# A check of the softmax sums moved onto TensorE, the zeros of two V tiles shared out, and a new written order

## The chip, the cores and the metric

The kernel runs on one core of one Trainium2 chip. The metric is the device time of one execution in microseconds; lower is better. The engines are TensorE (PE in the profile, its weight loads PEld), VectorE (DVE), ScalarE (ACT), GpSimd (POOL) and SyncE (SP, which issues nearly all DMAs).

## The reference

Two branches work on the same normalized input and are added to it:

```python
def _A_ref(x, wqkv, wo):            # attention: 32 heads of 16, window of 256 keys
    qkv = (x @ wqkv).reshape(B, S, 3, H, Dh).transpose(2, 0, 3, 1, 4)
    scores = einsum('bhqd,bhkd->bhqk', q, k) * Dh ** (-0.5)
    mask = (idx[:, None] - idx[None, :] >= 0) & (idx[:, None] - idx[None, :] < W)
    p = softmax(where(mask, scores, -1e9))
    return einsum('bhqk,bhkd->bhqd', p, v).transpose(0, 2, 1, 3).reshape(B, S, D) @ wo
def _B_ref(x, w_in, w_sp, b_sp, w_out):   # gated MLP with a mix over positions
    z = gelu(x @ w_in)
    z1, z2 = z[..., :Fh], layernorm(z[..., Fh:])
    g = einsum('ts,bsf->btf', w_sp, z2) + b_sp[None, :, None]
    return (z1 * g) @ w_out
xn = layernorm(x)
return x + _A_ref(xn, wqkv, wo) + _B_ref(xn, w_in, w_sp, b_sp, w_out)
```

S = 2048, D = 512, Fh = 688; all in bf16.

## The kernel before, in words

The tokens are 16 tiles of 128. A first part (to 83 us) normalizes x, makes z1 and z2 of all tiles and most of q, k and v. The part that matters here follows. It walks a string, `ORDER`, step by step, and issues for each step the instructions of all engines; each engine then runs its own in that sequence, held only by semaphores. So the string is the schedule. Its steps are:

- `q`, `g`, `f` and a number: begin the next qkv unit (4 matmuls of 512 columns), the next half tile of the position mix (`gf`, 16 matmuls of 344 columns, L588), or the next output tile (`fo`, 6 matmuls with uT and 4 with oT), and issue so many of its matmuls. A bare number goes on with the unit that is open.
- `S`: scores of one set, two PSUM score tiles of two banks each (`slot_mms`, L761), their exps by ScalarE into a tile `E` (L840) and the window masks by GpSimd's affine_select (L855). `A`, `B` and `T` do the same for three score tiles, the third copied by VectorE (L838), and open or close an output tile whose matmuls are issued one at a time by `y`.
- `D`: scores of the corners of the window (tile `ED`, L790); `d` masks them on VectorE (L862).
- `p`: P times V (`pv`, L727) for one block J of 256 queries and one group G of 8 heads, into a PSUM bank; VectorE turns it (`ot`, L734). `n` normalizes on VectorE: reciprocal of the sums into `r_all` (L740), product (L742), turn into `oT` (L750).

There are three score tiles in PSUM (`ps_s`), and two banks (`x_tile`) that gf, fo, o and the last qkv units share in turn. A bank comes free when VectorE has read it: into u (L602), xo (L627), ot (L734) or v_y (L168). uT comes from u by a DMA transpose, as do the weights wspT of tile t+2.

`pv` reads V through v_y, and for the corners through one of two tiles `vh0` and `vh1`, each loaded by two DMAs per block (`load_half`, L547 and L549) into half of its rows; the other half must be zero. `late()` closes the pool of xnT and the qkv weights, opens a pool in its place, and has GpSimd write these zeros (L539, L540). It is called by the first `D` or `p`.

The softmax is made without the maximum. At the end the kernel checks that every sum in `r_all` lies between 2^-60 and 2^40; if not, `attention_with_maximum` does the work again. `check_sums` counts the good sums of each partition (L873, L874), and a DMA brings the 128 counts into one row (L879). `least_sum`, called in `f_end` ahead of the last half tile's addition, takes the least of them (L886), and `make_flag` writes the flag (L892) after all steps. Every engine loads the flag into a register (L897) and branches (L1104). The last output tile is made in two halves of 256 columns; its second half is sent by ScalarE's queue.

Of the kernel before, what the change touches and what calls it, by code (L numbers as in the profile page):

```python
# [8 lines left out]
P = 128  # L9
BF = mybir.dt.bfloat16  # L10
F32 = mybir.dt.float32
ACT = mybir.ActivationFunctionType
ALU = mybir.AluOpType

S_TOK = 2048
D = 512
# [3 lines left out]
VROW = H * VW + DH  # L20
# [3 lines left out]
NB = S_TOK // P  # L24
NC = D // P
NG = 4
NJ = NB // 2
# [10 lines left out]
PAD = 64  # L38
# [4 lines left out]


ORDER = """
S q4 q2 S 2 q4 S q4 g7 D 9 S g10 S d 6 p S g5 n 11 D p p S p g7 D 5 n 3 d 1 g3 n 4 B y1 1 n y1 2
y1 3 y1 1 y1 2 A y3 g3 y1 5 d 2 B 5 y4 1 y2 A y1 g3 y1 2 y1 11 S p p D g12 S 4 n n g6 S 10 S p p
S g5 n 3 n 8 B y5 g1 y1 1 d y1 2 A 2 y1 5 y1 5 D p p D g4 n d 12 B n y2 g1 y1 1 y1 1 y1 3 A y1 1
y1 4 y1 1 y1 4 S p p S g8 n 6 d 2 B y4 g3 y1 1 n 3 A 1 y1 3 y3 5 D p p S g4 n 4 d 8 B y3 n g1 y1
3 y1 2 y1 A 1 y1 5 y2 4 D p p D g2 n 11 n 3 B y3 g3 d y1 1 y1 2 A 3 y2 1 y1 2 y1 4 S p p D g5 n  # L50
8 d 3 B y6 p A y2 d g11 y1 1 S 4 p n S p g6 n D 10 S p g6 n n 5 B y2 1 y1 3 y1 1 y1 d y4 T y8 n
y1 A g16 S p p D n g2 n 13 B y2 1 y4 d y3 T y9 A g16 D p p S g12 D d 4 g6 n S 8 n 2 S p p S g10
D n 4 n 2 f6 S 3 d 1 g7 S 9 S p p S g4 d 9 S n 3 g11 n 5 p p n f7 n 3 f10 f10 f10
"""


# [16 lines left out]
def kernel(  # L73
# [12 lines left out]
    nc = tc.nc  # L86
# [4 lines left out]
    pers = ctx.enter_context(tc.tile_pool(name="pers", bufs=1))  # L91
# [18 lines left out]
    xnT = pq.tile([P, NC, PAD + S_TOK], BF, name="xnT")  # L110
    wqkv = pq.tile([P, NC, 3 * D], BF, name="wqkv")
    r_all = pers.tile([P, NJ * NG, 16], F32, name="r_all")
    flag = pers.tile([P, 1], mybir.dt.int32, name="flag")
    wspp = ctx.enter_context(tc.tile_pool(name="wspp", bufs=2))
    sm = ctx.enter_context(tc.tile_pool(name="sm", bufs=4))
# [60 lines left out]
    with ExitStack() as actx:  # L176
        ps_s = actx.enter_context(
            tc.tile_pool(name="psa_s", bufs=2, space=bass.MemoryType.PSUM)
        )
# [49 lines left out]
        for w in WARM:  # L229
# [5 lines left out]
        nc.vector.memset(warm[:], 0.0)  # L235
        one = pa.tile([P, H], BF, name="one")
        nc.vector.memset(one[:], 1.0)
        nc.scalar.activation(out=warm[:, 0:4], in_=warm[:, 4:8], func=ACT.Gelu_apprx_tanh)
        make_identity(nc, ident[:])
        nc.vector.reduce_sum(  # L240
            out=hmask[:],
            in_=ident[:].rearrange("p (s e d) -> p e s d", s=4, e=2),
            axis=mybir.AxisListType.XY,
# [286 lines left out]
    def late():  # L530
        if not late_pool:
            assert not work["q"]
            pq_ctx.close()
            late_pool.append(
                late_ctx.enter_context(tc.tile_pool(name="late", bufs=1, side="right"))
            )
            for i in range(2):
                vh = late_pool[0].tile([P, 4, VROW], BF, name=f"vh{i}")
                nc.gpsimd.memset(vh[PAD:P, 0:2, :], 0.0)  # L539
                nc.gpsimd.memset(vh[0:PAD, 2:4, :], 0.0)  # L540
                v_half.append(vh)
        return late_pool[0]

    def load_half(J):
        late()
        vh = v_half[J % 2]
        nc.sync.dma_start(out=vh[0:PAD, 0:2, :], in_=v_y[0:PAD, 2 * J + 1 : 2 * J + 3, :])  # L547
        src = v_y[PAD:P, 2 * J - 2 : 2 * J, :] if J > 0 else v_y[0:PAD, 1:3, :]
        nc.sync.dma_start(out=vh[PAD:P, 2:4, :], in_=src)  # L549
# [72 lines left out]

    def f_end(t, c0, w, fo):
        xo = xos[t]
        if t == NB - 1 and c0 > 0:
            least_sum()
        nc.vector.tensor_tensor(  # L627
            out=xo[:, c0 : c0 + w], in0=fo[:, 0:w], in1=xo[:, c0 : c0 + w], op=ALU.add
        )
        eng = nc.scalar if c0 else nc.sync  # L630
        eng.dma_start(out=out2[t * P : (t + 1) * P, c0 : c0 + w], in_=xo[:, c0 : c0 + w])
        if not (rows or units or later):
            check_sums()
# [40 lines left out]
    def f_work(t, c0):  # L674
        if c0 == 0 and t + 2 < NB:
            load_xo(t + 2)
        w = f_cols(t)
        fo, _ = x_tile([P, 512], F32, "fo")
        for ch in range(NFC):
            nc.tensor.matmul(  # L680
                fo[:, 0:w], lhsT=uTs[t][:, ch, :], rhs=w_out_sb[:, ch, c0 : c0 + w],
                start=(ch == 0), stop=False,
            )
            yield
        q0 = t % 2 * P
        for c in range(NC):
            nc.tensor.matmul(  # L687
                fo[:, 0:w], lhsT=oTs[t // 2][:, c, q0 : q0 + P], rhs=wo_sb[:, c, c0 : c0 + w],
                start=False, stop=(c == NC - 1),
            )  # L690
            yield
        f_end(t, c0, w, fo)
# [75 lines left out]
    def do_corners(J, G):  # L768
        S = [ps_s.tile([P, 2, 512], F32, name="S", tag="S") for _ in range(2)]
        ED[(J, G // 2)] = late().tile([P, 32, PAD], BF, name="ED", bufs=2)  # L770
        if G == 0 and J == 0:
            load_half(0)
        if G == 2 and J + 1 < NJ:
            load_half(J + 1)
        Ed = ED[(J, G // 2)]
        for g in range(2):
            for t in range(2):
                i = 2 * J + t
                for strip in range(2):
                    late_q = strip == 0 or J == 0  # L780
                    k0 = i * P + P if late_q else i * P - 3 * PAD
                    q0 = i * P + PAD * late_q
                    gk = G + g + (2 * strip if J == 0 else 0)
                    for s in range(4):
                        o = S[s // 2][
                            strip * PAD : strip * PAD + PAD, s % 2, g * 256 : g * 256 + 256
                        ].rearrange("p (e t q) -> p e t q", e=2, t=2)[:, :, t, :]
                        score_mm(s, o, J, gk, k0, PAD, q0, PAD)
        for i in range(2):
            nc.scalar.activation(  # L790
                out=Ed[:, 16 * i : 16 * i + 16, :],
                in_=S[i][:].rearrange("p b (x q) -> p (b x) q", q=PAD),
                func=ACT.Exp, scale=SM_SCALE,
            )
# [73 lines left out]
    def check_sums():  # L868
        assert not (later or units)
        r = r_all[:].rearrange("p a b -> p (a b)")  # L870
        ok = ep.tile([P, 512], BF, name="ok", tag="E")
        low = ep.tile([P, 1], F32, name="low", tag="E")
        nc.vector.tensor_scalar(out=ok[:], in0=r, scalar1=R_LOW, scalar2=None, op0=ALU.is_ge)  # L873
        nc.vector.scalar_tensor_tensor(  # L874
            out=ok[:], in0=r, scalar=R_HIGH, in1=ok[:], op0=ALU.is_le, op1=ALU.mult,
            accum_out=low[:],
        )
        row = ep.tile([P, P], F32, name="row", tag="E")
        nc.sync.dma_start(out=row[0:1, :], in_=low[:])  # L879
        rows.append(row)  # L880

    lows = []

    def least_sum():
        low = sm.tile([P, 1], F32, name="low")
        nc.vector.tensor_reduce(  # L886
            out=low[0:1, :], in_=rows[0][0:1, :], axis=mybir.AxisListType.X, op=ALU.min
        )
        lows.append(low)

    def make_flag():
        nc.vector.tensor_scalar(  # L892
            out=flag[0:1, :], in0=lows[0][0:1, :], scalar1=16.0 * NJ * NG, scalar2=None, op0=ALU.is_lt
        )

    def read_flag():
# [177 lines left out]
    for step in ORDER.split():  # L1074
        if step in "STABCH":
            n = 2 if step == "S" else 1 if step == "H" else 3
            do_slots(n, step in "TA", step in "TB")
        elif step == "D":
            do_corners(*corners.pop(0))
        elif step == "d":  # L1080
            mask_corners(*masks.pop(0))
        elif step == "p":
            pv(*units.pop(0))
        elif step == "n":
            normalize(*later.pop(0))
        elif step[0] == "y":
            for _ in range(int(step[1:])):
                half_mm()
        else:
            if step[0] in work:  # L1090
                assert left == 0
                item = work[step[0]].pop(0)
                left, unit = (NFC + NC, f_work(*item)) if step[0] == "f" else item
                step = step[1:]
            for _ in range(int(step)):
                next(unit)
                left -= 1
            if left == 0:
                assert next(unit, None) is None
    assert not (left or slots or corners or masks or units or later or half)  # L1100
    assert not any(work.values())
    make_flag()
    late_ctx.close()
    with tc.If(read_flag() > 0):  # L1104
        with ExitStack() as gctx:
# [28 lines left out]
```

## Time and profile before

| | |
|---|---|
| Runs of the kernel before | 255.33, 255.51 and 256.52 us; median 255.51 |
| Profiled execution | 255.79 us, of which the span from the first to the last instruction is 254.0 |
| Busy | PE 247.7, ACT 195.6, DVE 200.1, POOL 105.3 us |
| TensorE clock granted | 0.999 |

A row of the chain of waits gives start, duration, engine, what it writes and its line; a row of the timeline adds shapes and a count, with the idle time before it and its releaser in square brackets. A row of the groups ends with busy time in us, mean ns of one, and idle time before. Matmuls overlap, so their recorded durations run past the start of the next; the distance from one stretch's start to the next one's is what the stretch costs.

### The profile page before, as it was taken

What the parts mean: (1) busy time and instruction counts of PE and PEld (TensorE: products, weight loads), DVE (VectorE), ACT (ScalarE), POOL (GpSimd) and SP (SyncE); (2) the same over time, 40 slices, a digit from 0 to 9 for tenths busy, and PEclk for the clock granted to TensorE, in tenths of its full rate; (3) what the DMA queues carried; (4) which work ended last, traced back from release to release, by engine and by line L of the source; (5) the groups of instructions that cost most, each with busy time, mean ns of one, the idle gap of its engine ahead of it and who ended that gap; (6) DMA issues with size and microseconds to landing.
All of it is one profiled execution on the core that took longest, in us unless ns stands there. A gap on an engine that the chain in (4) does not pass through costs nothing.

```text
span 254.0 us, 8684 instructions
## 1 busy us (share of the span) xinstructions
PE 247.7 (97%) x3712; PEld 141.3 (56%) x3712; DVE 200.1 (79%) x434; ACT 195.6 (77%) x234; POOL 105.3 (41%) x165
## 2 busy tenths in 40 slices
PE   7899999999999999999999999999999999999994
PEld 3555555555555356546557556566565464664653
DVE  7699977875657659985698898887998989684883
ACT  3756567556546998898989989889898899998900
POOL 3221211210010387575464465626484547543710
PEclk9999999999999999999999999999999999999999
DMA  6899722018400128646567717569184557675232
GB/s 198 291 252 195 195 54 31 1 41 104 105 1 0 44 46 122 143 124 137 54 86 181 131 44 189 50 157 157 38 168 41 138 77 126 117 101 125 36 54 69
DMA packets 67162, 26.82 MB, mean 106 GB/s; under 512 B 57040, under 2 KB 65584, under 8 KB 67120
## 3 DMA queue, kind: packets, MB, share of 16 engines
q1 hardware_dynamic: 66400, 25.50, 52.4%
q10 hardware_dynamic: 720, 0.73, 0.9%
q8 instruction: 30, 0.49, 0.9%
q14 instruction: 12, 0.10, 0.1%
HBM read 8.46 MB, written 2.10 MB: 42 GB/s over the span
## 4 chain that ended last, share of the span: by engine, by line
PE 92%; DMA 3%; DVE 2%; ACT 1%; issue 1%; SPq 0%; DVEq 0%
PE gf L588 31%; PE zp L370 14%; PE S L761 11%; PE fo L662 10%; PE o L727 9%; PE pj_o L143 6%; PE pj_f L143 5%; PE pj_o L161 3%; PE pj_f L161 2%; DMA w_in_sb<-in_B_w_in_dram 2%; DMA row<-low 1%; DVE xo L627 1%; PE fo L680 1%; PE zo L370 0%; PE fo L687 0%
## 5 line engine op out<-in xcount | busy, mean ns | idle before, releaser
L855 POOL TENSOR_SCALAR_AFFINE_SELECT E<-E 128x512 bf16<-128x512 bf16 x124 | 86.3, 721 | 68.0 <-ACT E L840 64.8
L840 ACT ACTIVATE E<-S 128x1024 bf16<-128x1024 f32 x102 | 97.6, 1027 | 9.1 <-PE S L761 9.0
L588 PE MATMUL gf<-z2n,wspT 128*128 128x344 bf16 x512 | 88.4, 310 | 0.0
L588 PEld LDWEIGHTS <-wspT 128*128 128x128 bf16 x512 | 47.4, 98 | 30.9 <-issue 5.9
L302 POOL TENSOR_TENSOR rs<-ve,mhalf 128x2 f32<-128x2 f32 (+1 forms) x18 | 12.1, 670 | 68.2 <-DVE ve L299 67.6
L370 PE MATMUL zp<-w_in_sb,xnT 128*128 128x344 bf16 x224 | 36.9, 309 | 0.1
L761 PE MATMUL S<-qpad,kT 32*64 32x128 bf16 (+2 forms) x848 | 32.0, 259 | 0.2 <-ACT E L840 0.2
L790 ACT ACTIVATE ED<-S 128x1024 bf16<-128x1024 f32 x30 | 29.1, 1024 | 1.6 <-PE S L761 1.5
L370 PEld LDWEIGHTS <-xnT 128*128 128x128 bf16 x224 | 21.6, 98 | 14.6 <-ACT xnT L361 0.7
L602 DVE SCALAR_TENSOR_TENSOR u<-gf,b_all,z 128x344 bf16<-128x344 f32 (+3 forms) x50 | 20.4, 438 | 11.7 <-PE gf L588 11.5
L734 DVE STREAM_TRANSPOSE ot<-o 128x512 f32<-128x512 f32 x32 | 22.5, 714 | 7.8 <-PE o L727 7.6
L838 DVE CAST E<-S 128x1024 bf16<-128x1024 f32 x22 | 26.7, 1213 | 2.2 <-PE S L761 2.2
L840 ACT ACTIVATE E<-E 128x1024 bf16<-128x1024 bf16 x22 | 23.4, 1063 | 0.8 <-DVE E L838 0.6
L727 PE MATMUL o<-E,v_y 128*32 128x128 bf16 (+1 forms) x736 | 23.5, 239 | 0.2
L761 PEld LDWEIGHTS <-kT 32*64 32x64 bf16 (+1 forms) x848 | 12.9, 99 | 18.6 <-issue 16.4
L727 PE MATMUL o<-ED,vh 128*32 128x64 bf16 x960 | 21.2, 193 | 0.0
L154 DVE TENSOR_SCALAR qpad<-qt,hmask 128x512 bf16<-128x512 bf16 x32 | 9.7, 348 | 13.6 <-ACT qt L152 13.6
L143 PEld LDWEIGHTS <-wqkv 128*128 128x128 bf16 x128 | 12.5, 98 | 12.8 <-DMA xnT<-xt 0.3
L862 DVE TENSOR_TENSOR ED<-ED,maskC 128x2048 bf16<-128x2048 bf16 x15 | 19.2, 1278 | 0.0
L378 ACT ACTIVATE z<-zp 128x688 bf16<-128x688 f32 x14 | 10.4, 743 | 10.9 <-PE zp L370 10.9
L143 PE MATMUL pj_o<-xnT,wqkv 128*128 128x512 bf16 x72 | 18.5, 379 | 0.0
L378 ACT ACTIVATE z2n<-zp 128x688 bf16<-128x688 f32 x14 | 10.4, 743 | 10.1 <-PE zp L370 10.1
(88 smaller groups left out, 306.7 us busy)
## 6 DMA issues: line engine op xcount, KB each, us to landing
vh<-v_y SPq DMA_DIRECT2D x16, 140.0 KB, 4.4
xo<-in_A_x_dram SPq DMA_DIRECT2D x16, 128.0 KB, 2.9
out_dram<-xo SPq DMA_DIRECT2D x15, 128.0 KB, 2.0
wqkv<-in_A_wqkv_dram SPq DMA_DIRECT2D x1, 1536.0 KB, 8.7
xt<-in_A_x_dram SPq DMA_DIRECT2D x2, 512.0 KB, 3.9
w_in_sb<-in_B_w_in_dram SPq DMA_DIRECT2D x5, 172.0 KB, 5.5
w_out_sb<-in_B_w_out_dram SPq DMA_DIRECT2D x1, 640.0 KB
w_in_sb<-in_B_w_in_dram ACTq DMA_DIRECT2D x3, 172.0 KB, 6.0
```

Source lines behind the costliest of these rows:

```text
L143: nc.tensor.matmul(pt[:], lhsT=wqkv[:, c, w0 : w0 + P], rhs=xnT[:, c, t0 : t0 + 512], start=(c == 0), stop=(c == NC - 1),)
L370: nc.tensor.matmul(out, lhsT=src[:, c, t0 : t0 + P], rhs=w_in_sb[:, c, f0 : f0 + HALF], start=(c == 0), stop=(c == NC - 1),)
L378: nc.scalar.activation(out=dst.rearrange("p (j f) -> p j f", j=2), in_=zp[:, :, 0:HALF], func=ACT.Gelu_apprx_tanh, scale=rsx[n] if n < 2 e ...
L588: nc.tensor.matmul(gf[:, 0:HALF], lhsT=wspT[t][:, c, :], rhs=z2n[:, c, j * HALF : (j + 1) * HALF], start=(c == 0), stop=(c == NB - 1),)
L662: nc.tensor.matmul(h["fo"][:], lhsT=lhsT, rhs=rhs, start=False, stop=(h["jobs"] == 2 and h["pos"] == NFH))
L727: nc.tensor.matmul(o[32 * s : 32 * s + 32, c0 + r0 : c0 + r0 + n], lhsT=v[:, m, h * VW : h * VW + 32], rhs=rhs(s), start=(i == 0), stop=(i ...
L734: nc.vector.transpose(out=ot[:].rearrange("p b j -> p (b j)"), in_=o[:])
L761: nc.tensor.matmul(out, lhsT=kT[32 * s : 32 * s + 32, g, k0 : k0 + nk], rhs=qpad[J // 2][32 * s : 32 * s + 32, g, :, qs - q00 : qs - q00 + ...
L790: nc.scalar.activation(out=Ed[:, 16 * i : 16 * i + 16, :], in_=S[i][:].rearrange("p b (x q) -> p (b x) q", q=PAD), func=ACT.Exp, scale=SM_ ...
L838: nc.vector.tensor_copy(out=part, in_=src)
L840: nc.scalar.activation(out=part, in_=src, func=ACT.Exp, scale=SM_SCALE)
L855: nc.gpsimd.affine_select(out=cells[:, :, k, :], in_=cells[:, :, k, :], pattern=pattern, compare_op=op, fill=0.0, base=base, channel_multi ...
```

## The change

- The row transfer and the least are gone. `check_sums` makes a column `bad` of 128 ones and zeros, and `make_flag` is called within the last half output tile, between its six uT matmuls and its four oT matmuls: a matmul with `bad` as weights and a column of ones counts the bad partitions into one element of a score tile, and VectorE compares that with 0.5.
- The zeros of vh0 are written by VectorE when `late()` opens the pool, those of vh1 by GpSimd at the corner step of block 1. `late()` is called when the last qkv unit is done.
- The string is another one, with the same units in another sequence.

```diff
 ORDER = """
-S q4 q2 S 2 q4 S q4 g7 D 9 S g10 S d 6 p S g5 n 11 D p p S p g7 D 5 n 3 d 1 g3 n 4 B y1 1 n y1 2
-y1 3 y1 1 y1 2 A y3 g3 y1 5 d 2 B 5 y4 1 y2 A y1 g3 y1 2 y1 11 S p p D g12 S 4 n n g6 S 10 S p p
-S g5 n 3 n 8 B y5 g1 y1 1 d y1 2 A 2 y1 5 y1 5 D p p D g4 n d 12 B n y2 g1 y1 1 y1 1 y1 3 A y1 1
-y1 4 y1 1 y1 4 S p p S g8 n 6 d 2 B y4 g3 y1 1 n 3 A 1 y1 3 y3 5 D p p S g4 n 4 d 8 B y3 n g1 y1
-3 y1 2 y1 A 1 y1 5 y2 4 D p p D g2 n 11 n 3 B y3 g3 d y1 1 y1 2 A 3 y2 1 y1 2 y1 4 S p p D g5 n
-8 d 3 B y6 p A y2 d g11 y1 1 S 4 p n S p g6 n D 10 S p g6 n n 5 B y2 1 y1 3 y1 1 y1 d y4 T y8 n
-y1 A g16 S p p D n g2 n 13 B y2 1 y4 d y3 T y9 A g16 D p p S g12 D d 4 g6 n S 8 n 2 S p p S g10
-D n 4 n 2 f6 S 3 d 1 g7 S 9 S p p S g4 d 9 S n 3 g11 n 5 p p n f7 n 3 f10 f10 f10
+S q4 q4 q1 S 3 q4 D g8 S 8 g1 S 2 d 9 S 4 p S p g4 n 4 S 8 p D p g9 D 6 n 1 g2 n 6 B y1 3 y3 n 5
+y1 A y2 g2 y2 3 d 5 B 1 y1 2 y2 1 y1 2 y3 A g5 y1 5 y1 6 S p d p S g9 n 3 S 4 g6 S 6 n 4 D p p S
+g14 n 1 n 1 B y5 g2 d 3 y1 1 A y2 2 y1 8 D p p D g6 n n 10 B y2 g2 y1 2 d 4 y1 A y2 2 y1 1 y1 1
+y1 4 S p n p S g11 n 5 B y3 d g1 y1 1 y1 2 y1 A 4 y1 3 y1 1 y1 4 D p p S g10 n 3 n 3 B y2 g1 y1
+6 d y1 2 A y2 1 y2 2 y1 4 D p p D g7 n n 9 B y2 g1 y1 1 d y2 3 y1 A 3 y2 4 y1 4 S p p D g15 d 1
+B y4 n y1 p A y3 g4 y1 3 d 6 S 3 p n n S p g5 S 11 D p g5 n 2 d 2 B 4 y2 3 y6 n y1 T y6 n y3 A
+g16 S p p n D g4 n 11 B y1 1 y8 T y1 d y8 A g16 D p p S g2 n 1 d 9 n 1 D 3 g6 S 10 S p p S g4 n
+9 D 1 d 2 d g5 S 7 n 4 f2 S 8 S p n p S g4 n 7 S 5 p g11 n 5 p f4 n 6 f10 f10 f10
 """
...
+    one1 = pers.tile([P, 1], BF, name="one1")
...
+        nc.vector.memset(one1[:], 1.0)
...
             for i in range(2):
-                vh = late_pool[0].tile([P, 4, VROW], BF, name=f"vh{i}")
-                nc.gpsimd.memset(vh[PAD:P, 0:2, :], 0.0)
-                nc.gpsimd.memset(vh[0:PAD, 2:4, :], 0.0)
-                v_half.append(vh)
+                v_half.append(late_pool[0].tile([P, 4, VROW], BF, name=f"vh{i}"))
+            clear_half(nc.vector, 0)
         return late_pool[0]
+
+    def clear_half(eng, i):
+        eng.memset(v_half[i][PAD:P, 0:2, :], 0.0)
+        eng.memset(v_half[i][0:PAD, 2:4, :], 0.0)
...
     def f_end(t, c0, w, fo):
         xo = xos[t]
-        if t == NB - 1 and c0 > 0:
-            least_sum()
...
             yield
+        if c0 > 0:
+            make_flag()
         q0 = t % 2 * P
...
         if G == 0 and J == 0:
             load_half(0)
+        if G == 0 and J == 1:
+            clear_half(nc.gpsimd, 1)
...
-        row = ep.tile([P, P], F32, name="row", tag="E")
-        nc.sync.dma_start(out=row[0:1, :], in_=low[:])
-        rows.append(row)
-
-    lows = []
-
-    def least_sum():
-        low = sm.tile([P, 1], F32, name="low")
-        nc.vector.tensor_reduce(
-            out=low[0:1, :], in_=rows[0][0:1, :], axis=mybir.AxisListType.X, op=ALU.min
-        )
-        lows.append(low)
+        bad = ep.tile([P, 1], BF, name="bad", tag="E")
+        nc.vector.tensor_scalar(
+            out=bad[:], in0=low[:], scalar1=16.0 * NJ * NG, scalar2=None, op0=ALU.is_lt
+        )
+        rows.append(bad)
 
     def make_flag():
+        count = ps_s.tile([P, 2, 512], F32, name="S", tag="S")[0:1, 0, 0:1]
+        nc.tensor.matmul(count, lhsT=rows[0][:], rhs=one1[:], start=True, stop=True)
         nc.vector.tensor_scalar(
-            out=flag[0:1, :], in0=lows[0][0:1, :], scalar1=16.0 * NJ * NG, scalar2=None, op0=ALU.is_lt
+            out=flag[0:1, :], in0=count, scalar1=0.5, scalar2=None, op0=ALU.is_ge
         )
...
             if left == 0:
                 assert next(unit, None) is None
+                if not work["q"]:
+                    late()
     ...
     assert not any(work.values())
-    make_flag()
```

## Prediction

> **What bounds the kernel now.** I read the page first: the span and the chain that ended last.
>
> ```profile
> span 254.0 us, 8684 instructions
> ...
> PE 92%; DMA 3%; DVE 2%; ACT 1%; issue 1%; SPq 0%; DVEq 0%
> PE gf L588 31%; PE zp L370 14%; PE S L761 11%; PE fo L662 10%; PE o L727 9%; PE pj_o L143 6%; PE pj_f L143 5%; PE pj_o L161 3%; PE pj_f L161 2%; DMA w_in_sb<-in_B_w_in_dram 2%; DMA row<-low 1%; DVE xo L627 1%; PE fo L680 1%; PE zo L370 0%; PE fo L687 0%
> ```
>
> The reader is to see that 92% of the chain is TensorE. A written order can then gain in only three ways: TensorE does less, TensorE waits less, or what comes after its last matmul gets shorter. So I looked in the chain of waits for the pieces that show what a stretch costs when nothing holds it. A score visit is one letter S of the order; a PV visit is one or two p in a row; the rest is full-array matmuls.
>
> ```profile
> 91.52 0.33 PE S L761 x4
> ...
> 117.29 1.46 PE o L727 x112
> ...
> 121.29 1.56 PE gf L588 x10
> ...
> 126.87 2.44 PE gf L588 x16
> ...
> 188.23 0.79 PE o L727 x56
> ...
> 198.70 2.05 PE fo L662 x9
> ```
>
> A gf matmul costs (2.44 - 1.56)/6 = 0.147 us, and a stretch of them has 1.56 - 1.47, some 0.1 us, on top. That is the change between full-array and tiled matmuls. An fo or qkv matmul is (2.05 - 0.1)/9 = 0.217. Two PVs together take 1.46 and one alone 0.79, so the second costs 0.67 and each visit some 0.12 beside its matmuls. Priced like this, most of the old order between 100 and 240 us comes out with nothing left over: TensorE hardly waits there. Its waits are at the two ends of the attention.
>
> ```profile
> 83.56 1.47 PE L161 MATMUL pj_f<-wqkv,xnT 128*128 128x512 bf16 x6
> 84.96 0.39 PE L761 MATMUL S<-qpad,kT 32*128 32x512 bf16 x2
> 85.53 0.39 PE L761 MATMUL S<-qpad,kT 32*128 32x512 bf16 x2 [0.19 <-ACT E L840]
> ```
> ```profile
> 87.33 0.43 PE S L761 x8
> ...
> 98.46 1.16 PE o L727 x64
> 99.62 0.40 PE S L761 x4
> 100.01 0.56 PE o L727 x32
> ```
>
> The second S visit began at 84.96, and half of it had to wait to 85.53 for the first exp, which frees a score buffer: 0.57 lost. The third took 0.43 in place of 0.33 (0.1). At 98.46 two first-block PVs take 1.16; one takes 0.56, so the two should take 0.56 + 0.56 - 0.12 = 1.00, and 0.16 is waiting; the next S has 0.07 more. GpSimd explains these two, in the timeline:
>
> ```profile
> 91.59 1.03 POOL L539 MEMSET vh<- 64x1120 bf16 x1
> ...
> 95.80 3.88 POOL L855 TENSOR_SCALAR_AFFINE_SELECT E<-E 128x512 bf16<-128x512 bf16 x6
> ```
>
> The four zero fills start at 91.59, with the masks next at 95.80: three sets stand queued behind the fills until 99.68, just what those PVs read. At the other end the pair of last PVs is held once more, and then the row transfer decides:
>
> ```profile
> 242.13 0.85 PE o L727 x56
> ...
> 243.01 0.90 PE o L727 x56
> ...
> 248.72 1.93 DMA row<-low
> ...
> 250.68 0.28 DVE low L886
> ```
>
> From 242.13 to 243.91 is 1.78, against 1.46 for a free pair: 0.3.
>
> **The change, part by part.** *The order on TensorE, own work.* All letters but the run of the p are as many as before. Counted in the two orders, p p stands 13 times before and 11 after, so the PVs are made in 21 visits and not 19, and the two extra ones cut full-array stretches in two. Each costs 0.12 + 0.1: **+0.45**.
>
> *The order, waits.* After the first S the new order puts nine qkv matmuls and not six: 83.56 + 9 x 0.217 + 0.1 = 85.61, later than 85.53, where the buffer comes free, so the 0.57 goes. The third use is now the corner step D, after 3 + 4 matmuls (1.6 us) where six stood; the 0.1 goes as well. What is late next is the bank of the qkv tiles, which a cast on VectorE frees; that goes into the new waits below. The PVs of block 0 come one by one behind S or D, with no zero fills ahead of their masks: -0.23. The final pair is parted by 11 gf matmuls (1.6 us, more than the turn of o on VectorE): -0.3. Sum **-1.2**.
>
> A small wait in the middle has a plain cause, and I have no reason to think that a tight order has fewer of them:
>
> ```profile
> 184.71 1.68 DVE L862 TENSOR_TENSOR ED<-ED,maskC 128x2048 bf16<-128x2048 bf16 x1
> ...
> 187.04 0.12 PEld L727 LDWEIGHTS <-v_y 128*32 128x32 bf16 x8 [0.43 <-DVE xo L627]
> ```
> ```profile
> L862 DVE TENSOR_TENSOR ED<-ED,maskC 128x2048 bf16<-128x2048 bf16 x15 | 19.2, 1278 | 0.0
> ```
>
> A mask of 1.68 in place of the mean 1.28 made an xo late, and with it the bank of the next PV. The new order packs exps, masks and turns as closely elsewhere: I add 0.2 (between 0 and 1) for waits that did not exist.
>
> *Zeros of the V tiles.* Buffer 0 is cleared by VectorE as soon as the last qkv unit is evicted, buffer 1 by GpSimd at the corner of block 1.
>
> ```profile
> L260 DVE MEMSET v_y<- 64x272 uint32 x1 | 0.3, 285 | 0.0
> ```
> ```profile
> 88.76 1.40 DVE L168 CAST v_y<-pj_f 64x512 bf16<-64x512 f32 x2 [0.70 <-PE pj_f L161]
> 91.56 0.58 DVE L602 SCALAR_TENSOR_TENSOR u<-gf,b_all,z 128x344 bf16<-128x344 f32 x1 [1.41 <-PE gf L588]
> ```
>
> 1120 bf16 elements are 560 words, 2.06 times the 272 of the row: 0.6 us each, or 1.2 if they are written one by one. Two of them are 1.2 to 2.4 us behind the last casts. VectorE idles 1.41 there before the first u, and that u's bank is wanted only a whole gf unit later (2.44), so I take nothing; queued behind the clears are the first u and the first corner mask, and without that cover a clear would cost up to 1.0. The wait of the clears, for the last read of xnT, is the one of the casts just ahead. The two fills left on GpSimd stand where its queue waits for exps: nothing. The fill of the ones column, one more small memset on VectorE while the first loads are in flight, is nothing too.
>
> *Count and flag.* Gone are a 1.93 us transfer, the reduce, and the wait behind both; new are one compare on VectorE (as short as the flag's), a one-column matmul and the flag from PSUM. The matmul's place is TensorE's path. Its nearest rows are a visit's extra, 0.12 + 0.1 if it drains the array, and next to nothing if it goes in the stream: 0 to 0.22, I take **+0.1**. The Trainium skill, TensorEngine Tiling (Array Packing), section Instruction Overhead, says that a one-column matmul lasts as long as one of 60 columns; as an estimate from that page it would be 0.03 at its clock, and the sum 0.07 less. No row here has one column.
>
> What the end wins is read here:
>
> ```profile
> 248.79 0.60 PE L687 MATMUL fo<-wo_sb,oT 128*128 128x256 bf16 x4
> ...
> 249.34 1.01 SPq L631 DMA_DIRECT2D out_dram<-xo  x2
> 249.43 0.42 DVE L627 TENSOR_TENSOR xo<-fo,xo 128x256 bf16<-128x256 f32 x1 [0.27 <-PE fo L687]
> ...
> 249.88 0.60 PE L687 MATMUL fo<-wo_sb,oT 128*128 128x256 bf16 x4
> ...
> 250.88 0.40 DVE L627 TENSOR_TENSOR xo<-fo,xo 128x256 bf16<-128x256 f32 x1
> 251.21 0.13 DVE L892 TENSOR_SCALAR flag<-low 1x1 int32<-1x1 f32 x1
> 251.31 0.36 ACTq L631 DMA_DIRECT2D out_dram<-xo  x1
> ```
> ```profile
> out_dram<-xo ACTq DMA_DIRECT2D x1, 64.0 KB, 1.6
> ```
> ```profile
> L897 SPq TENSOR_LOAD <-flag x1: 478/478/478, 251.4 to 251.4; - x1
> ```
> ```profile
> L1129 SPq EVENT_SEMAPHORE  x10: 17/28/28, 252.7 to 254.0; - x10
> ```
>
> After the first half's last matmul (249.39) its xo starts within 0.04. The second half's PE ends at 250.48 and xo starts at 250.88, held by the row's reduce: 0.36 late. So out goes at 250.95 and lands at 252.55, not 252.9. The flag, now counted before the last four matmuls, is there by about 250.3, while SyncE is free at 249.34 + 1.01 = 250.35; its load, branch and closing list come a whole us earlier, and the list then stands waiting for that landing. It started at 252.7 before, with eight waits some 0.06 apart, and passed the landing at about 253.15. Now it passes at 252.55 to 252.6: **-0.6** (no less than 0, no more than 1.0, the whole shift of the flag).
>
> *Sum*: 0.45 - 1.2 + 0.2 + 0.1 - 0.6 = -1.05. Of the new waits' 0 to 1, more lies above my 0.2 than below it, so I round to **-0.9**. The profiled execution took 255.79 (254.0 span and 1.8 around it), so it would be 254.9; the median of the runs is 255.51, 0.28 below, and gives **254.6**.
>
> **The rivals.** *Only the end.* The waits taken away at 85 and 98 us come back later, because ScalarE, busy 91% of the stretch below, sets the pace from there; the order then wins nothing, and 255.51 - 0.6 + 0.1 + 0.2 = 255.2. For it: ScalarE has little room. Against: TensorE waited for it after 95 us nowhere in the timeline.
>
> ```profile
> 170.00:195.00 25.00, 24.92 (x568) 14.96 (x568) 21.90 (x39) 22.87 (x24) 14.22 (x21) 1.00 0.62 99
> ```
>
> (Busy time of PE, PEld, DVE, ACT, POOL: 22.87 of 25 is 91% for ScalarE.)
>
> *All waits gone.* No new wait comes, the one at 187.04 goes too (0.2 of the 0.43, as some of it is the change of tiling), the count is free: 0.45 - 1.2 - 0.2 - 0.6 = -1.55, 254.0. For it: the new order keeps its nine matmuls and its lone PVs just where the old one waited. Against: nothing shows that the middle gets looser.
>
> *Slower: VectorE late at the banks.* If masks and normalizations meet GpSimd's selects more often, each late xo or u holds a bank and TensorE with it. At 1.68 a mask is 0.4 over its mean, and the row at 187.04 shows how it gets to TensorE. Past the middle of the 15 masks, with 8 of them 0.4 late and all of that on TensorE, it costs 3.2 and the time is 255.51 - 0.9 + 3.2 = 257.8; it decides from six masks (2.2 in all brings the time over 256.8). For it: the mean of 1278 shows that it happens. Against: of 15 masks one clear case reached TensorE. The Trainium skill, SBUF — State Buffer, section Who interferes with whom, states that a VectorE instruction with two SBUF inputs and a GpSimd instruction that reads SBUF exclude each other for their whole length; the 1.68 beside selects fits it.
>
> *It doesn't do what it says.* The count or the flag comes after the last xo, and the end keeps its length: 255.51 - 0.3 = 255.2; I count it with the first rival.
>
> **How the numbers follow.** The bound for a difference that a measurement of this kernel can tell is 0.5%, 1.28 us: faster is below 254.23, slower above 256.79. Forecast 0.55, only the end (and no shorter end) 0.17, all waits gone 0.18, banks 0.10. The forecast's own spread (its added waits 0 to 1, count 0 to 0.22) is 254.1 to 255.4, and a tenth of it lies below 254.23: faster 0.18 + 0.06 = 0.24, slower 0.10, the same 0.66. The range is 253.7 to 255.9: it leaves out the banks and the low tail.
>
> **What would show it.** Right: no row transfer in the profile; the second S visit of the attention starts without a wait on ScalarE; PVs in 21 visits; one tiny matmul among the last fo, and the flag written before the last xo; the last xo within 0.1 of its matmul; 2.9 us from the last matmul's end to the span's end, not 3.5. Wrong: a wait of TensorE on VectorE's u, xo or turn of o, repeated over the blocks; a clear on VectorE that holds the first u; the flag last on VectorE again.

## The result, and the profile after

The changed kernel takes 257.38 us (median of 8 runs, 256.52 to 258.09), the kernel before 255.83 (8 runs, 255.33 to 256.52): a ratio of 1.0063 [1.0042, 1.0084]. 254.6 was forecast, 253.7 to 255.9 as the range. An execution over 1.5% above its kernel's fastest is left out of the ratios, which concerns two of the six of shift_64 below and no others. The profiled execution took 257.02 (255.79 before). From the page of the kernel after:

```profile
span 255.3 us, 8657 instructions
...
PE 94%; DMA 2%; issue 1%; ACT 1%; SPq 0%; DVE 0%
...
L868 DVE TENSOR_TENSOR ED<-ED,maskC 128x2048 bf16<-128x2048 bf16 x15 | 18.7, 1244 | 0.9 <-ACT ED L796 0.9
```

The row transfer has left the chain (DMA 3% before, 2% now), the masks are no longer than before (1244 ns), and still the span is 1.3 longer. Two anchors divide it: the first score visit of the attention and the last matmul. The first, before and after, in the timelines of TensorE:

```profile
83.23 0.40 PE L761 MATMUL S<-qpad,kT 32*128 32x512 bf16 x4
```
```profile
82.72 0.40 PE L765 MATMUL S<-qpad,kT 32*128 32x512 bf16 x4
83.05 2.31 PE L162 MATMUL pj_f<-wqkv,xnT 128*128 128x512 bf16 x8
85.29 0.40 PE L765 MATMUL S<-qpad,kT 32*128 32x512 bf16 x4
```

After, the second score visit (85.29) runs its four matmuls in one piece, where half of it had waited for ScalarE. At the end, all engines:

```profile
249.09 0.82 PE L682 MATMUL fo<-w_out_sb,uT 128*128 128x256 bf16 x6
...
249.84 0.16 PE L892 MATMUL S<-one,bad 128*1 128x1 bf16 x1
...
249.94 0.61 PE L691 MATMUL fo<-wo_sb,oT 128*128 128x256 bf16 x4
250.04 0.14 DVE L893 TENSOR_SCALAR flag<-S 1x1 int32<-1x1 f32 x1 [0.33 <-PE S L892]
250.58 0.42 DVE L629 TENSOR_TENSOR xo<-fo,xo 128x256 bf16<-128x256 f32 x1 [0.40 <-PE fo L691]
251.04 0.36 ACTq L633 DMA_DIRECT2D out_dram<-xo  x1
```

The last matmul ends at 249.94 + 0.61 = 250.55 (250.48 before). So the span splits like this:

| stretch (us) | before | after | change | forecast |
| --- | --- | --- | --- | --- |
| start to first score visit | 83.23 | 82.72 | -0.5 | 0 |
| first score visit to last matmul's end | 167.25 | 167.83 | +0.6 | -0.45 |
| last matmul's end to span end | 3.5 | 4.75 | +1.2 | -0.6 |

The start carries no edit that could shorten it and varied from 82.3 to 84.8 over the runs shown here; it is scatter. The other two lines are the loss.

**The middle** holds a stop that was not there before. Timeline of TensorE, then of its weight loads, in the kernel after:

```profile
128.30 0.60 PE L765 MATMUL S<-qpad,kT 32*128 32x512 bf16 x4
129.38 0.39 PE L765 MATMUL S<-qpad,kT 32*128 32x256 bf16 x3 [0.48 <-issue]
129.92 0.81 PE L664 MATMUL fo<-w_out_sb,uT 128*128 128x512 bf16 x3 [0.16 <-issue]
```
```profile
129.37 0.11 PEld L765 LDWEIGHTS <-kT 32*128 32x128 bf16 x3 [0.97 <-issue]
```

In the middle of one score visit TensorE gets no instruction for almost a microsecond, and the releaser is "issue": no semaphore, no engine. Against the prices of the prediction this visit is 0.84 late.

**The end**: the flag is counted a microsecond earlier, as meant, and SyncE's load of it too (250.2, from 251.4). But SyncE then stands. Its queue's waits, before and after, and its closing list in the kernel after:

```profile
SPq L897 <- DVE flag L892: 1.0, 1, 1.0
```
```profile
SPq L1131 <- DMA out_dram<-xo: 2.3, 1, 2.3
```
```profile
L898 SPq TENSOR_LOAD <-flag x1: 584/584/584, 250.2 to 250.2; - x1
```
```profile
L1131 SPq DRAIN  x3: 7/7/13, 254.5 to 254.8; - x3
```

It waits 2.3 us for an output that ScalarE had issued at 251.04, 0.27 earlier than before. The DMA view shows why. Each line holds 40 slices of 0.075 us from 251.5 on; before, and then after:

```profile
GB/s 0 0 0 0 0 0 0 0 0 150 287 273 144 21 0 0 0 0 0 0 109 218 109 0 109 0 0 0 0 0 0 0 0 0 0 0 0 0 0 0
```
```profile
GB/s 0 0 0 0 0 68 335 485 157 48 0 0 109 0 7 27 20 0 0 0 109 0 0 0 7 7 14 7 7 14 0 0 0 0 0 0 0 0 0 0
...
q10 hardware_dynamic: 144, 0.07, 8.2%
q14 instruction: 3, 0.02, 3.5%
q8 instruction: 1, 0.02, 2.6%
```

109 GB/s in one slice is a packet of 8 KB, 218 one of 16 KB, 7 one of 512 B. Before, the output goes in one burst (252.2 to 252.5), and four packets of the kind "instruction", code, follow after it (253.0 on). After, the code comes into the burst (251.95 to 253.5 in the packet records; the 16 KB one lasts 1.25 us, 0.97 before), and single output packets of 512 B still start at 253.6. The output lands 3.3 us after its issue, against 1.6. Of its 16 landings in the trace, 14 come by 252.64 and the other two at 253.39 and 254.37, so two parts of it are late, not the whole.

### The profile page after: what moved, and what is told of

The parts are those of the page before. It is cut to its first block, busy times and chain, and to the rows that moved or that the text cites. A ratio compares the mean times of both kernels' runs of the same rounds, so it can differ in the third digit from the quotient of the medians.

```text
span 255.3 us, 8657 instructions
## 1 busy us (share of the span) xinstructions
PE 246.0 (96%) x3692; PEld 140.7 (55%) x3713; DVE 199.8 (78%) x437; ACT 196.1 (77%) x234; POOL 104.3 (41%) x163
## 4 chain that ended last, share of the span: by engine, by line
PE 94%; DMA 2%; issue 1%; ACT 1%; SPq 0%; DVE 0%
PE gf L592 31%; PE zp L372 14%; PE S L765 11%; PE o L731 9%; PE fo L664 9%; PE pj_o L144 6%; PE pj_f L144 5%; PE pj_f L162 3%; PE pj_o L162 3%; DMA w_in_sb<-in_B_w_in_dram 2%; PE fo L682 2%; PE fo L691 1%; PE zo L372 0%; ACT z2n L380 0%; SPq L200 0%
## 5 line engine op out<-in xcount | busy, mean ns | idle before, releaser
L861 POOL TENSOR_SCALAR_AFFINE_SELECT E<-E 128x512 bf16<-128x512 bf16 x124 | 87.2, 728 | 69.2 <-ACT E L846 67.1
L868 DVE TENSOR_TENSOR ED<-ED,maskC 128x2048 bf16<-128x2048 bf16 x15 | 18.7, 1244 | 0.9 <-ACT ED L796 0.9
```

The source lines that it names most:

```text
L861: nc.gpsimd.affine_select(out=cells[:, :, k, :], in_=cells[:, :, k, :], pattern=pattern, compare_op=op, fill=0.0, base=base, channel_multi ...
```

## The experiments

Theory A: the flag's branch, taken past the block that is left out, loads code from far away; with the flag early these loads meet the last output, which the closing list waits for. Theory D, formed from the stop at 129: TensorE stands at the end of a block of its own code and waits for the next. The rivals stand in the expectations. Ratios are to the kernel before on the same chip.

### flag_late: the changed kernel, flag compared after the last xo

```diff
     def make_flag():
         ...
+        counts.append(count)
+
+    def set_flag():
         nc.vector.tensor_scalar(
-            out=flag[0:1, :], in0=count, ...
+            out=flag[0:1, :], in0=counts[0], ...
...
     assert not any(work.values())
+    set_flag()
```

> The changed kernel with one thing moved: VectorE writes the flag after the last addition to xo, not before it; the one-column matmul stays where it is. Theory A (code loading): with the early flag the engines branch about 1 us sooner, and the blocks of code that they then load (8 and 16 KB) share the DMA engines with the last 64 KB of output, so this lands 3.3 us after its issue and not 1.6. With the flag late the output should land within 1.8 us of its issue again, the stretch from TensorE's last matmul to the span's end should fall from 4.7 to about 3.3 us, and the time from 257.4 to about 256.0. Rival B (the order alone is slower, the slow landing is chance): the time stays within 0.4 of 257.4, and the landing varies whatever the flag does.

255.45 us, ratio 0.9982 [0.9955, 1.0009], span 253.7. Its end in the timeline, and its DMA from 251.5:

```profile
250.51 0.42 DVE L629 TENSOR_TENSOR xo<-fo,xo 128x256 bf16<-128x256 f32 x1 [0.87 <-PE fo L691]
250.85 0.14 DVE L898 TENSOR_SCALAR flag<-S 1x1 int32<-1x1 f32 x1
250.97 0.36 ACTq L633 DMA_DIRECT2D out_dram<-xo  x1
```
```profile
GB/s 0 0 0 0 82 225 314 192 62 0 0 0 0 0 0 109 218 0 0 0 0 109 0 109 0 0 0 0 0 0 0 0 0 0 0 0 0 0 0 0
```

The output is issued at the same place of the work, but the code packets come after it again (252.6 on), and SyncE has no wait for the landing in its list. A flag 0.8 us later makes the kernel 1.9 us faster (2.1 by the two ratios).

### old_order_new_flag, old_order_flag_late, new_order_old_flag: the halves apart

The first is the kernel before with only the count matmul and the early flag, the second the same with `set_flag()` as above, the third the changed kernel with the row transfer, reduce and flag of before.

```diff
 # old_order_new_flag, against the kernel before (ORDER and zeros stay)
-            least_sum()
...
+        if c0 > 0:
+            make_flag()
...
-        nc.sync.dma_start(out=row[0:1, :], in_=low[:])
+        bad = ep.tile([P, 1], BF, name="bad", tag="E")
...
-    make_flag()
```

> The kernel before with only the new count and the early flag (old string, old zeros). Theory A: the slow landing comes with the flag: output lands 3 us or more after issue, the end is 1.2 us longer, TensorE has 0.2 more for the count: about 257.1. Rival B: the order is not there, so the time is 255.4 to 255.8.

> The kernel before with the new count, the flag written after the last addition (old string, old zeros). Theory A: no slow landing, the last addition 0.36 us earlier than before, the count costs 0.2: 255.5 to 255.8, within 0.3 of the kernel before. Rival B: the same, 255.4 to 255.8; this one sets the price of the count by itself.

> The changed kernel (new string, new zeros) with the old row transfer, least and flag. Theory A: the end is as before (3.5 us after the last matmul); what is left is the order: 0.45 more own work of TensorE, 1.3 of old waits gone, and the 0.84 that TensorE stood still near 129 us for its own code. 255.4 if that halt was chance, 256.2 if it comes each time. Rival B: 257.0 or more.

| kernel | order, zeros | flag | us | ratio |
| --- | --- | --- | --- | --- |
| old_order_new_flag | old | counted, early | 257.52 | 1.0057 [1.0032, 1.0082] |
| old_order_flag_late | old | counted, late | 255.86 | 1.0009 [0.9987, 1.0030] |
| new_order_old_flag | new | row transfer | 255.58 | 0.9983 [0.9958, 1.0007] |

The loss goes with the early flag under either order. The waits of SyncE's queue in old_order_new_flag show the same wait for the landing as the kernel after:

```profile
SPq L1129 <- DMA out_dram<-xo: 2.5, 1, 2.5
```

The old order with a late counted flag is level with the kernel before: taking the row transfer off the end gains nothing that these runs can tell. In the profiles its tail is 0.36 shorter than before (3.18, from 3.54), but its stretch from the first score visit to the last matmul is 0.6 longer (167.88, from 167.25): the count, and some 0.3 of waiting ahead of the last half tile's matmuls. The new order, with either late flag, is 0.2% better in the median, with 1 inside both intervals.

### no_branch: the early flag without the branch

The flag is counted early and loaded as in the changed kernel; the conditional block (attention_with_maximum, which handles sums out of range) is left out.

```diff
-    with tc.If(read_flag() > 0):
-        with ExitStack() as gctx:
-            attention_with_maximum(gctx)
+    read_flag()
```

> The changed kernel with its early flag, which every engine still loads, but without the conditional block behind it: the second computation of the attention, and so the jump over it, is left out. Theory A (the jump makes the engines load far code, whose 8 and 16 KB blocks share the DMA engines with the last output): no such blocks at the end, output lands 1.6 us after issue, 255.2 or less. Rival C (the five early loads of the flag, not the code, slow the output): landing still 3 us, 257 or more.

254.98 us, ratio 0.9980 [0.9964, 0.9995]. Its DMA queues from 250 to 254 hold no code, and the output, issued at 250.45, is through in one burst:

```profile
q10 hardware_dynamic: 144, 0.07, 5.6%
q1 hardware_dynamic: 139, 0.06, 5.4%
```

The last matmul ends at 249.95 and the span at 253.0: 3.05, where 2.9 was forecast for the early flag. So it is the branch's code, not the early compare or the load of the flag. That this code is the cause is shown; that it works by sharing the DMA engines with the output is read from the packet records, and no run tests it by itself.

### flag_late_old_zeros: the four fills back on GpSimd

```diff
 # against flag_late, in late(), for i in range(2)
-                v_half.append(late_pool[0].tile([P, 4, VROW], BF, name=f"vh{i}"))
-            clear_half(nc.vector, 0)
+                vh = late_pool[0].tile([P, 4, VROW], BF, name=f"vh{i}")
+                nc.gpsimd.memset(vh[PAD:P, 0:2, :], 0.0)
+                nc.gpsimd.memset(vh[0:PAD, 2:4, :], 0.0)
+                v_half.append(vh)
```

> The changed kernel with the flag late and the four zero fills on GpSimd again, at the first corner step. By the prediction's reading the third set's mask then stands behind 4.1 us of fills, and the first PV, which came right behind that mask, waits 0.5 to 1.5 us: 256.0 to 256.9. If the zeros' place is worth nothing: 255.4.

255.53 us, ratio 1.0000 [0.9984, 1.0017], against 0.9982 for flag_late: less than expected, and no difference that the two intervals can tell. The trace shows a cost all the same: a PV visit is held until 94.20, as the first mask behind the fills ends, and loses 0.34. The profiled execution hides part of it, as its stop at 129 is shorter than that of flag_late (0.61 between the starts of two weight loads, against 0.84). GpSimd's timeline has the masks behind the fills again:

```profile
92.36 1.02 POOL L542 MEMSET vh<- 64x1120 bf16 x1
...
93.49 5.10 POOL L861 TENSOR_SCALAR_AFFINE_SELECT E<-E 128x512 bf16<-128x512 bf16 x8
```

### shift_64 and shift_120: more warm-up matmuls ahead

The kernel starts with ten matmuls on a tile that nobody reads. Each is two TensorE instructions (a weight load and a matmul), so their number shifts the whole later program by so many instructions and leaves its work as it is.

```diff
 # against flag_late
-WARM = [512] * 8 + [32] * 2
+WARM = [512] * 5 + [32] * 37    # shift_64: 64 instructions more
+WARM = [512] * 3 + [32] * 67    # shift_120: 120 more
```

> The changed kernel with the flag late, and the warm-up of TensorE made of 42 matmuls and not 10 (three of the large ones given for 35 small ones): 64 more instructions ahead of everything, nothing else. Theory D (the halt of 0.6 to 0.85 us near 129 us is TensorE waiting for its own next block of code, which comes in blocks of 16 KB): the blocks end at other places of the string, so the halt moves or goes; gone, the time is 254.8, else up to 255.5. Rival E (it is a transfer or a bank that this place of the string waits for): the halt stays at the same matmul, 255.4.

> The same with 70 warm-up matmuls, 120 more instructions. Theory D: the halt moves or goes once more, and another may come elsewhere, 254.7 to 255.6. Rival E: at the same matmul, 255.4.

261.57 us, ratio 1.0198 [1.0166, 1.0231], and 262.70, ratio 1.0271 [1.0232, 1.0309]: some 5 and 7 us lost by the ratios, with nothing changed after the first 5 us. Neither theory had forecast such a loss: D had said 255.6 at most. But the stop has moved, against rival E. In shift_64 it comes 32 matmuls earlier in the work, in a PV visit, which is the 64 instructions of the shift; in both runs others have come. Both profiled executions (264.5 and 264.1) are longer than the medians, so only the places of the stops are read from them. TensorE in shift_64, then in shift_120:

```profile
125.96 0.23 PE L731 MATMUL o<-ED,vh 128*32 128x64 bf16 x6
128.55 0.21 PE L731 MATMUL o<-ED,vh 128*32 128x64 bf16 x2 [2.37 <-issue]
```
```profile
137.24 0.31 PE L765 MATMUL S<-qpad,kT 32*64 32x128 bf16 x14
139.39 0.35 PE L765 MATMUL S<-qpad,kT 32*64 32x128 bf16 x18 [1.84 <-issue]
```

### shift_256, shift_16, shift_240, before_shift_64: is it the block of 256?

```diff
 # the first three against flag_late, the last against the kernel before
-WARM = [512] * 8 + [32] * 2
+WARM = [32] * 138               # shift_256
+WARM = [512] * 7 + [32] * 11    # shift_16
+WARM = [512] * 2 + [32] * 128   # shift_240
+WARM = [512] * 5 + [32] * 37    # before_shift_64
```

> The flag_late kernel with 138 short warm-up matmuls (32 columns) ahead of the work instead of 10, 256 more TensorE instructions, a whole block of code. Theory D (TensorE halts at the ends of its code blocks of 256 instructions): every block end falls on the same matmul as in flag_late, so the only halt over 0.5 us after 80 us is again the one in the second quarter of the span, at the first score visit after a 5-pair PV step, and from the first score visit to the last output's matmul it takes the 167.6 us of flag_late within 0.5; time 255.4 to 256.5 (the longer warm-up may put the first matmuls back by up to 0.8 us). Rival (more warm-up instructions cost by their number, or the warm-up's shape does it): the halts and the loss grow with the count, beyond the 6 to 7 us of 64 and 120 instructions, 262 or more.

> The flag_late kernel with 18 warm-up matmuls instead of 10 (7 of 512 columns, 11 of 32): 16 more TensorE instructions ahead, so each block of code ends 16 instructions earlier in the work. Theory D: the halt of 0.84 us at 129 moves to a matmul 16 instructions earlier or goes, others may come; without any it would be 254.6, with the one as it is 255.45, so 254.4 to 256.5. Rival (place does not matter): 255.45 within 0.3 and the halt at the same matmul.

> The flag_late kernel with 130 warm-up matmuls instead of 10 (2 of 512 columns, 128 of 32): 240 more TensorE instructions, so each block of code ends 16 instructions later in the work than in flag_late. Theory D: as for shift_16 in the other direction; 254.6 with no halt, 255.45 with one of the same size, and up to 0.8 us more where the longer warm-up puts the first matmuls back: 254.4 to 257. Rival (more instructions cost by their number): 262 or more.

> The kernel before, with its own order, zeros, row transfer and flag, and the 42 warm-up matmuls of shift_64 (64 more TensorE instructions ahead). Theory D: the kernel before has no halt only because its block ends happen to fall where the next block is there already; moved by 64 instructions it halts too, by 2 to 8 us in all: 258 to 264. Rival (the halts belong to the new order): no halt over 0.5 us beside the old wait at the second score visit, 255.8 within 0.5.

| kernel | us | ratio | stop near 128 |
| --- | --- | --- | --- |
| shift_256 | 256.09 | 1.0019 [1.0002, 1.0036] | the same matmul of the score visit |
| shift_16 | 255.34 | 0.9990 [0.9968, 1.0012] | 16 instructions earlier, in gf |
| shift_240 | 255.05 | 0.9969 [0.9955, 0.9984] | none |
| before_shift_64 | 260.67 | 1.0172 [1.0136, 1.0208] | none there, two others |

The timelines of TensorE around 128 us, of shift_256, shift_16 and shift_240:

```profile
128.53 0.60 PE L765 MATMUL S<-qpad,kT 32*128 32x512 bf16 x4
129.29 0.39 PE L765 MATMUL S<-qpad,kT 32*128 32x256 bf16 x3 [0.16 <-issue]
```
```profile
127.04 0.89 PE L592 MATMUL gf<-z2n,wspT 128*128 128x344 bf16 x5
128.47 0.46 PE L592 MATMUL gf<-z2n,wspT 128*128 128x344 bf16 x2 [0.53 <-issue]
```
```profile
128.34 0.60 PE L765 MATMUL S<-qpad,kT 32*128 32x512 bf16 x7
129.10 1.03 PE L664 MATMUL fo<-w_out_sb,uT 128*128 128x512 bf16 x4 [0.16 <-issue]
```

With 256 more instructions the stop is between the same two matmuls as in the kernel after (the x4 and the x3 of one score visit), and the 5 to 7 us of shift_64 and shift_120 are not there: not the number of instructions costs, but their place modulo 256. With 16 more it comes eight matmuls earlier, which is 16 instructions. And the kernel before, shifted by 64, stops too. Its TensorE, and the clock in two of its stretches (PEclk is the third number from the end):

```profile
158.67 0.28 PE L761 MATMUL S<-qpad,kT 32*128 32x256 bf16 x2
161.28 0.39 PE L761 MATMUL S<-qpad,kT 32*128 32x256 bf16 x6 [2.33 <-issue]
```
```profile
163.00:170.00 7.00, 6.84 (x47) 3.44 (x47) 3.62 (x7) 4.31 (x6) 2.54 (x4) 0.84 0.22 45
170.00:180.00 10.00, 9.84 (x239) 6.10 (x238) 8.77 (x16) 9.27 (x11) 4.16 (x6) 1.00 0.66 115
```

Counted in program order over all these kernels, every gap of more than 0.55 us between the starts of two weight loads after 90 us (19 gaps, in ten kernels; the other four have none) ends with the instruction that follows number 193 or 194 modulo 256. Four of the 19 (0.56 to 0.70, near 160) stand where the new order has a gap of 0.40 even when no block ends there, so only the rest of these is the block's. The kernel after has some 7,450 instructions on TensorE and 30 code packets of 16 KB on queue q8, about one for every 256. Theory D is shown: TensorE stops where one block of its code ends. The old order is not better here; it only stands so that none of its block ends falls badly.

The Trainium skill, Runtime: NRT & Kernel Launch, section Instruction fetch mechanics, agrees on the size, blocks of 256 instructions that the sequencer fetches by itself, and on the branch, which it says has to fetch its target when that is not in the window. It calls the crossing of a block mostly hidden; here one crossing cost up to 2.4 us of standing still, and the measurement decides.

## Why the prediction was wrong, by its own steps

**Own work, removed waits, count: right in sum.** shift_240 has the changed kernel's order, zeros and count, and no stop. Its anchors in the timeline:

```profile
82.76 0.40 PE L765 MATMUL S<-qpad,kT 32*128 32x512 bf16 x4
...
249.00 0.61 PE L691 MATMUL fo<-wo_sb,oT 128*128 128x256 bf16 x4
```

From 82.76 to 249.61 is 166.85, against 167.25 before: -0.40. The steps for this stretch (0.45 - 1.2 + 0.2 + 0.1) gave -0.45. Laid beside shift_240 weight load by weight load, the kernel after falls 0.85 back at the stop at 129 and 0.14 at the block end at 160.7, and nowhere else by more than 0.08: the two block ends are the whole difference of 0.98. PVs are made in 21 visits, as counted. By the prices of the prediction, the waits at the second and third score use, behind the fills and at the last pair are gone in the kernel after, and some 0.4 us is left beside the stop (the largest is 0.17 at 85, for the qkv bank that VectorE frees, as named); no run measures these terms one by one. The last pair is parted by 16 gf matmuls, not 11, as the 5 behind the `n` belong to the same unit; that favours the term.

**The count matmul** was mis-sized within its range: the first matmul behind the count starts at 249.94 and would have been due at 249.75 without it, so 0.19 where 0.1 was taken. The end named for a drain of the array (0.22) is the nearer one; the 0.03 estimated from the Trainium skill, TensorEngine Tiling (Array Packing), section Instruction Overhead, is not borne out.

**Zeros: right.** The removed wait behind the fills was put at 0.23; with the fills on GpSimd again (flag_late_old_zeros) it is 0.34. VectorE's clears take 0.53 each, on words, and end before the first u, which again waits for its matmuls:

```profile
88.80 0.53 DVE L545 MEMSET vh<- 64x560 uint32 x1
89.48 0.53 DVE L546 MEMSET vh<- 64x560 uint32 x1 [0.15 <-issue]
90.57 0.58 DVE L606 SCALAR_TENSOR_TENSOR u<-gf,b_all,z 128x344 bf16<-128x344 f32 x1 [0.57 <-PE gf L592]
```

**New waits, +0.2 (0 to 1): wrong in kind.** It was argued from VectorE's masks and banks. What came was 0.84 in one piece, from no engine and no semaphore; that it lies inside the 0 to 1 is luck. With the 0.14 at 160.7 it is the way from the -0.40 of shift_240 to the +0.58 of the kernel after.

**The end, -0.6 (no less than 0, no more than 1.0): the step that failed.** Its premises held: the flag was written at 250.04 (about 250.3 was forecast), the last xo began within 0.04 of its matmul, out was issued 0.27 earlier. It then let the output land after the usual 1.6 us and the list pass at once. But what SyncE and the other engines do after the branch is not only waiting: they load code over the DMA engines that carry the output. The profile of before showed those packets at 253.0 to 254.1, behind the output, under "q8" and "q14" of the kind "instruction"; the prediction moved the branch past the output and did not move its DMAs with it. A tail of 4.75 in place of 2.9 is 1.85 of the miss, and flag_late gets 1.9 back. The bound "no less than 0" had no ground.

**The rivals.** "Slower: VectorE late at the banks" gave 257.8, close to the 257.38 measured, and is not what happened: the masks average 1244 ns, less than before, and no wait on VectorE repeats over the blocks. "Only the end" has it the wrong way round: the order gains (shift_240) and the end loses. "It doesn't do what it says" fell as well: count and flag come where they should.

**A version that was faster than both**: shift_240, the best of six places that were tried for the block ends, with the new order and zeros, the count matmul, the flag after the last xo and 130 warm-up matmuls: 255.05, 0.9969 [0.9955, 0.9984] of the kernel before. Its advantage hangs on where the blocks of code end and may not outlast the next edit.

## What to carry to other kernels

Work that is taken off the critical path can release something else earlier, so a branch, a wait or a load that now comes first has to be followed with all its transfers, code included, up to what the program's end waits for. When TensorE stands with "issue" as the releaser in the middle of one visit, count its instructions modulo 256 before blaming a new order: a shift by a few dummy instructions is a test of one line, and what it shows can be larger than what the edit was for. And two orders are compared fairly only at several such shifts.

## What the runs showed of the hardware that was not expected

- 64 dummy instructions ahead of the work, done within the first 5 us, cost the kernel before 4.4 us and the new order 5.5 by the ratios (before_shift_64 1.0172; shift_64 1.0198, against 0.9982 for flag_late). The profiles show a few stops in each, of up to 2.6 us between the starts of two weight loads.
- A long stop can cost more than its length: in the profiled execution of before_shift_64, after the 2.33 at 158.7, the granted clock is 0.84 from 163 to 170 (0.50 from 161.8 to 165.2 and 1.00 from there on), and the next steps are 4.3 us late in all by the prices of the prediction. It need not: after the 2.37 at 126 in shift_64 the clock stays at 1.00. Four of the six executions of before_shift_64 had a mean granted clock of 1.000 and still took 258.5 to 261.3, so most of that loss is not the clock. What decides is not shown.
- In 15 of the 19 gaps TensorE goes on 1.3 to 1.5 us after the end of the 16 KB code packet in the records; in the four small ones near 160 it is 2.4 to 3.0 (in the kernel after, the packet lasts from 126.72 to 127.87 and the next weight load starts at 129.37). In the kernel before, the packet for the block end of the same number lasts from 125.46 to 127.41, and TensorE gets there at 129.26, 1.85 later: in time. Two PVs are 112 matmuls, 224 instructions in 1.46 us, so nearly a block goes by in little more than a fetch lasts. What makes the fetch start late is open: in the kernel after it starts at 126.72, as the transposition of wspT (issued at 123.09) is about to leave the DMA engines, but no run took the transpositions away.
